# GpSimd's work of the later pairs on VectorE, and M1's two halves a step apart in an attention kernel with two feed-forward layers

## The chip, the cores and the metric

The kernel runs on one core of a Trainium2 chip. The metric is device time in microseconds (us), the median of several executions.

## What is computed

An attention over channels feeds two feed-forward layers. `q`, `k` and `v` are 6016 x 256, the hidden width is 2048.

```python
qn = q / (np.linalg.norm(q, axis=1, keepdims=True) + 1e-06)
kn = k / (np.linalg.norm(k, axis=1, keepdims=True) + 1e-06)
a = softmax(kn.transpose(0, 2, 1) @ qn / tau)     # 256 x 256
x = v @ a
h = x @ w_in;  x = (h * np.clip(h + 3.0, 0.0, 6.0) / 6.0) @ w_out
h = x @ w_in2; r = np.maximum(h, 0.0); out = (r * r) @ w_out2
```

## The kernel before

**Products.** Every product of float32 data is made of three passes (`passes`, lines 308 to 310): an operand is split into a high part (a cast on ScalarE) and a low part (operand minus high part, a subtraction); high times high, low times high and high times low are accumulated in PSUM. The part that is subtracted is called the remainder below.

**Weights.** `v @ a` is never formed: M1 = `a @ w_in` (256 x 2048) is made on the chip and takes the place of the first weights. M1 is made in four parts of 512 hidden columns (`c4` = 0 to 3), each of two halves (`m1_part(c4, i)`, one half of the 256 channels each: six matmuls into a PSUM bank `mp`, then ScalarE's high and VectorE's low parts by `m1_out`, lines 474 and 475). `m1_keep` (line 483) copies both banks out for sums that are formed later.

**Pairs.** The 6016 tokens go in pairs of token groups of 512 (the last pair: 448): pair (j, p), layer j = 0 or 1, p = 0 to 5. The first pair, (0, 0), runs in 32 plain steps of 12 matmuls, in which the parts of M1 and the weights of layer 0 are made ready as well. Step `a` uses part `a // 8` of M1. A part was made at step `x = a + M1_LEAD`, `x` a multiple of 8, both halves one behind the other, that is at steps 6, 14 and 22, and the products that need it are issued at steps 7, 15 and 23.

**Strassen.** The other eleven pairs form the first product of the layer by Winograd's seven products (`strassen`), in eight units (u) of 256 hidden columns. A unit has 45 matmuls: 7 products and 8 groups of the second product, each of three passes. The products need sums and differences of the input blocks (`T1` to `T4`, line 708), split in high and low parts (`hi`, line 711, and `lo`, line 715): eleven GpSimd instructions for each pair, made by `prepare` during the pair before. The weights need such sums too (`m1_sum`, `combine`, line 214; `m1_sums_split`).

**Second weights.** While layer 0 runs, the weights of layer 1 come as 64-bit floats, are converted (`from_float64`, five stages on ScalarE and VectorE, lines 152 to 165), summed (line 214), split (lines 239 to 244 and line 123) and written to DRAM, one `prepare_in` and one `prepare_out` for each u. The sums and remainders were GpSimd's.

**Order.** The program order on each engine is written by hand. `at(place, go)` puts a step at a place; 15 places (`SLOTS`) are one unit of three matmuls a place, place 0 is where the first Strassen pair begins, and `run` issues the steps in order of place. `on_pool` moves a step on until no other GpSimd step lies within 3.2 places:

```python
def on_pool(place, go):
    while any(abs(place - x) < POOL_APART for x in taken):
        place += 0.3
```

In each unit VectorE has eleven instructions of its own: adds of PSUM and a copy (line 761, `h`), the activation (line 775 or 780, `g`) and the remainders (line 123 by way of `split`, `gs`). PE waits for them at fixed places: the first remainder is issued at place 13.8 of a unit and used at 18, the second 17.8 and 21, the third 20 and 24, the fourth 23.4 and 27; the add at 12.6 must have read bank `q` before the product at place 16 adds to it. All engines work through their lists in order. SP issues every transfer.

Of the kernel before, what the change touches and what calls it, by code (L numbers as in the profile page):

```python
# [32 lines left out]
BUSY = (6, 2, 2, 3)  # L33
M1_LEAD = 2
EARLY = 12
# [5 lines left out]
SIGN = -(2 ** 31)  # L41
POOL_APART = 3.2
SLOTS = 15
# [10 lines left out]
def attention_then_two_ffns(  # L54
# [62 lines left out]

    def split(hi, lo, x, part=2, rest=None):

        if part != 1:  # L120
            nc.scalar.copy(hi, x)  # L121
        if part != 0:
            (rest or nc.vector).tensor_tensor(out=lo, in0=x, in1=f32(hi), op=ALU.subtract)  # L123

# [81 lines left out]

    def combine(i, st, a, b):
# [104 lines left out]
    with tc.manual_schedule():  # L312
# [166 lines left out]
        def m1_keep(c4):  # L479
            for k in range(KC):  # L480
                if k == 0:
                    m32[c4] = spare(2 * c4 + 1, f"m32_{c4}").rearrange("p (k f) -> p k f", k=KC)
                nc.scalar.activation(m32[c4][:, k, :], mps.pop((c4, k)), AF.Copy, scale=rsum[k])

        m1_st = {}

        def m1_sum(c4, i):

            if i == 0:
                m1_st[c4] = spare(2 * c4, f"st{c4}").rearrange("p (u a c) -> p u a c", u=2, a=4)  # L490
            m = [m32[c4][:, k, :].rearrange("p (u f c) -> p u f c", u=2, f=2) for k in range(KC)]
            combine(i, m1_st[c4], [[t[:, :, f, :] for f in range(2)] for t in m], lambda t, i: t[:, :, i, :])
# [171 lines left out]

        def on_pool(place, go):
# [12 lines left out]
        def prepare(j, p, start, end):  # L678
# [15 lines left out]
            def combination(r):  # L694
# [18 lines left out]
            def lo(r):  # L713
                h, l = operands[j, p, r]
                nc.gpsimd.tensor_tensor(out=l, in0=ts[r], in1=f32(h), op=ALU.subtract)  # L715

            at(start, load)
            when = {B11: 18.3, B21: 22.3, T2: 26.3}
            for i, r in enumerate((T1, T2)):
                on_pool(start + 12 + 4 * i, lambda r=r: combination(r))  # L720
            for r, x in when.items():
                at(start + x, lambda r=r: hi(r))
                on_pool(start + x + 1.7, lambda r=r: lo(r))
            for i, r in enumerate((T3, T4)):
# [121 lines left out]
        def load_wo2(u):  # L846
            wo_of[u] = wo_tile(u, "wo2_")
            nc.sync.dma_start(out=f32(wo_of[u]), in_=wo2_d[u])

        def prepare_in(u, begin):  # L850
            made = []
            at(begin, lambda: made.extend(second_in(u)))
            for i, x in enumerate((8.7, 9.5, 17.3, 19.4, 22.4)):
                at(begin + x, lambda i=i: made[0][i]())
            x = begin + 22.4
            for i in range(4):
                x = on_pool(x + 3, lambda i=i: made[1](i))
            at(x + 4, lambda: made[2]())
            for i in range(2):
                x = on_pool(x + 6 - 2 * i, lambda i=i: made[3](i))  # L860
            at(x + 6, lambda: made[4]())

        def prepare_out(u, begin):
            made = []
            at(begin, lambda: made.extend(second_out(u)))
            for i, x in enumerate((8.7, 9.5, 17.3, 19.4)):
                at(begin + x, lambda i=i: made[0][i]())
            at(begin + 22.4, lambda: made[0][4](0))
            x = on_pool(begin + 24.5, lambda: made[0][4](1))
            at(x + 6, lambda: made[1]())  # L870
# [83 lines left out]
```

## Time and profile before

| | us |
|---|---|
| median of 3 runs (1062.21 to 1064.5) | 1064.21 |
| the profiled execution | 1063.71 |
| its span, first to last instruction | 1061.9 |
| PE busy | 1042.6 |
| VectorE (DVE) busy | 864.2 |
| ScalarE (ACT) busy | 664.6 |
| GpSimd (POOL) busy | 251.4 |

The span runs from the first to the last instruction of the profiled execution; 1.8 us of its time lie outside. Busy times of matmuls are modelled and overlap; the start of a matmul minus the start of the one before it tells more. Names: acc, y, x, q, h, mp are PSUM banks, gs the split activation, L123 a line of the kernel.

### The profile page before, as it was taken

Reading aid. Unit: us, or ns where it says so; the run is one execution under the profiler, and the core shown is the slowest. Engines: PE = TensorE matmul, PEld = TensorE weight load, DVE = VectorE, ACT = ScalarE, POOL = GpSimd, SP = SyncE. Lnnn points to the kernel's source line nnn. Section 1 sums busy time; section 2 is a strip of 40 time slices with the busy share of each in tenths; the row PEclk is TensorE's granted clock in tenths of the full one; section 3 lists DMA queues with packets and bytes.
Section 4 is the critical chain, followed back from the end, with each engine's and each line's share of the span. In section 5 each row is a group of like instructions: output and inputs, shape, how many; then the busy total and the mean of one; then the engine's idle time right before and its main releaser. Section 6 shows DMA issues by size and latency. Waiting matters only on the chain.

```text
span 1061.9 us, 13045 instructions
## 1 busy us (share of the span) xinstructions
PE 1042.6 (98%) x4630; PEld 865.0 (81%) x4630; DVE 864.2 (81%) x1283; ACT 664.6 (63%) x1200; POOL 251.4 (24%) x211
## 2 busy tenths in 40 slices
PE   9999999999999999999999999999999999999998
PEld 8867777887877888787998888888888888888997
DVE  7898867898898889888889678678778878778766
ACT  6777767777777778776777445455445445545443
POOL 0012244343134133324233022113103104103000
PEclk9999999999999999999999999999999999999999
DMA  9911203102302301320765100100200200200100
GB/s 352 349 42 40 80 1 120 55 20 95 119 0 102 137 31 40 115 90 0 243 236 211 49 1 36 44 1 6 74 1 1 80 1 0 75 1 1 40 1 35
DMA packets 25938, 77.65 MB, mean 73 GB/s; under 512 B 2833, under 2 KB 4881, under 8 KB 25873
## 3 DMA queue, kind: packets, MB, share of 16 engines
q1 hardware_dynamic: 25872, 76.82, 20.4%
q8 instruction: 36, 0.59, 0.2%
q14 instruction: 30, 0.24, 0.1%
HBM read 52.95 MB, written 23.86 MB: 72 GB/s over the span
## 4 chain that ended last, share of the span: by engine, by line
PE 78%; DVE 14%; ACT 6%; issue 2%; POOL 0%; ACTq 0%; POOLq 0%
PE acc L310 13%; PE acc L308 13%; PE acc L309 13%; PE y L308 6%; PE y L309 6%; PE y L310 6%; DVE gs L123 4%; PE s L298 4%; PE q L308 3%; PE q L309 3%; PE q L310 3%; DVE g L775 3%; PE x L308 2%; PE x L310 2%; PE x L309 2%
## 5 line engine op out<-in xcount | busy, mean ns | idle before, releaser
L123 DVE TENSOR_TENSOR gs<-g,gs 128x512 fp32r<-128x512 f32 (+1 forms) x384 | 293.2, 764 | 71.3 <-ACT gs L784 61.7
L310 PE MATMUL acc<-gs,wo 128*128 128x512 f32 (+1 forms) x768 | 298.2, 388 | 5.1 <-DVE gs L123 5.0
L308 PE MATMUL acc<-gs,wo 128*128 128x512 f32 (+1 forms) x768 | 296.6, 386 | 1.6 <-ACT gs L121 1.0
L309 PE MATMUL acc<-gs,wo 128*128 128x512 f32 (+1 forms) x768 | 296.0, 385 | 0.0
L784 ACT CAST gs<-g 128x512 fp32r<-128x512 f32 (+1 forms) x352 | 208.5, 614 | 79.5 <-DVE g L775 55.9
L310 PEld LDWEIGHTS acc<-gs,wo 128*128 128x128 f32 x768 | 144.1, 188 | 39.9 <-DVE gs L123 12.9
L308 PEld LDWEIGHTS acc<-gs,wo 128*128 128x128 f32 x768 | 144.3, 188 | 29.9 <-ACT gs L121 2.2
L309 PEld LDWEIGHTS acc<-gs,wo 128*128 128x128 f32 x768 | 144.3, 188 | 26.7
L715 POOL TENSOR_TENSOR x<-raw,x 128x512 fp32r<-128x512 f32 (+1 forms) x55 | 73.1, 1330 | 368.6 <-ACT x L711 367.1
L780 DVE SCALAR_TENSOR_TENSOR g<-h 128x512 f32<-128x512 f32 (+1 forms) x144 | 120.5, 837 | 0.0
L761 DVE TENSOR_TENSOR h<-q,se 128x512 f32<-128x512 f32 (+1 forms) x88 | 59.5, 676 | 64.3 <-ACT se L757 64.3
L757 ACT COPY se<-y 128x512 f32<-128x512 f32 (+1 forms) x88 | 50.6, 575 | 92.5 <-PE y L310 92.2
L775 DVE SCALAR_TENSOR_TENSOR g<-r,h 128x512 f32<-128x512 f32 (+1 forms) x120 | 104.5, 871 | 3.5 <-ACT r L767 2.9
L757 ACT COPY su<-y 128x512 f32<-128x512 f32 (+1 forms) x88 | 50.8, 577 | 87.4 <-PE y L310 77.1
L767 ACT ACTIVATE r<-h,three 128x512 f32<-128x512 f32 (+1 forms) x120 | 85.6, 714 | 12.5 <-DVE h L761 12.2
L769 ACT ACTIVATE r<-y 128x512 f32<-128x512 f32 (+1 forms) x48 | 28.3, 590 | 56.7 <-PE y L310 56.6
L761 DVE TENSOR_TENSOR h<-q,su 128x512 f32<-128x512 f32 (+1 forms) x88 | 59.2, 673 | 1.0
L761 DVE TENSOR_TENSOR h<-x,sa 128x512 f32<-128x512 f32 (+1 forms) x88 | 59.1, 672 | 0.0
L757 ACT COPY sa<-y 128x512 f32<-128x512 f32 (+1 forms) x88 | 50.7, 576 | 7.0 <-PE y L310 0.9
L780 DVE SCALAR_TENSOR_TENSOR g<-y,r 128x512 f32<-128x512 f32 (+1 forms) x48 | 32.5, 677 | 19.9 <-ACT r L769 19.6
L298 PE MATMUL s<-qk 128*128 128x256 f32 x188 | 42.8, 389 | 0.0
L298 PEld LDWEIGHTS s<-qk 128*128 128x128 f32 x188 | 36.4, 196 | 5.5 <-DMA qk<-in_qk 0.6
(234 smaller groups left out, 1856.8 us busy)
## 6 DMA issues: line engine op xcount, KB each, us to landing
qk<-in_qk SPq DMA_DIRECT2D x23, 512.0 KB, 7.4
wo<-in_w_out SPq DMA_DIRECT2D x16, 512.0 KB, 5.8
wi<-in_w_in SPq DMA_DIRECT2D x10, 512.0 KB, 4.9
x2d<-o SPq DMA_DIRECT2D x20, 256.0 KB, 2.6
raw<-x2d SPq DMA_DIRECT2D x10, 512.0 KB, 5.8
out<-o SPq DMA_DIRECT2D x20, 256.0 KB, 2.3
raw<-in_vt SPq DMA_DIRECT2D x8, 512.0 KB, 6.4
wo2d<-wo2s SPq DMA_DIRECT2D x8, 512.0 KB, 3.0
```

The costliest lines, as they stand in the source:

```text
L123: (rest or nc.vector).tensor_tensor(out=lo, in0=x, in1=f32(hi), op=ALU.subtract)
L298: nc.tensor.matmul(s_ps[i], lhsT=x[:, C + i * P:C + (i + 1) * P], rhs=x[:, :C], start=(t == 0), stop=(t == NT - 1))
L308: nc.tensor.matmul(ps, lhsT=ah, rhs=bh, start=first, stop=False, skip_group_check=more)
L309: nc.tensor.matmul(ps, lhsT=al, rhs=bh, start=False, stop=False, skip_group_check=more)
L310: nc.tensor.matmul(ps, lhsT=ah, rhs=bl, start=False, stop=last, skip_group_check=more)
L715: nc.gpsimd.tensor_tensor(out=l, in0=ts[r], in1=f32(h), op=ALU.subtract)
L757: nc.scalar.copy(s[tag], s["y"])
L761: nc.vector.tensor_tensor(out=s[which], in0=s[ps], in1=s[tag], op=ALU.add)
L767: nc.scalar.activation(s["r" + which], h, AF.Relu, bias=three)
L775: nc.vector.scalar_tensor_tensor(out=g, in0=s["r" + which], scalar=6.0, in1=h, op0=ALU.min, op1=ALU.mult)
L780: nc.vector.scalar_tensor_tensor(out=g, in0=h, scalar=0.0, in1=r, op0=ALU.max, op1=ALU.mult)
L784: nc.scalar.copy(gs[which][0], s["g" + which])
```

## The change

The steps that were GpSimd's go to VectorE, except the sums of parts 0 and 1 of M1 and the operands of pair (0, 1). Of GpSimd's 201 two-input instructions 178 move, 23 stay. They are kept 2.6 places apart in place of 3.2 (3.2 up to place 0). The sums of parts 2 and 3 of M1 begin at places 10 and 34, no longer at -9 and 17. The second weights of u begin at (3.5 + 4.05 u) units in place of (2 + 4.5 u), those of the output at (5.5 + 4.05 u) in place of (4.25 + 4.5 u), and their stages stand closer. With `M1_LEAD` 3 and `x = a + M1_LEAD - i` the first half of a part is made at steps 5, 13 and 21, the second at 6, 14 and 22 as before. No instruction is added or left out on any engine beside the move.

```diff
-M1_LEAD = 2
+M1_LEAD = 3
-POOL_APART = 3.2
+APART = 2.6
+APART_FIRST = 3.2
...
-        nc.gpsimd.tensor_tensor(out=b(st, to), in0=x, in1=y, op=op)
+        eng.tensor_tensor(out=b(st, to), in0=x, in1=y, op=op)
...
-            nc.gpsimd.tensor_tensor(out=lo[:, a, :], in0=w, in1=f32(hi[:, a, :]), op=ALU.subtract)
+            nc.vector.tensor_tensor(out=lo[:, a, :], in0=w, in1=f32(hi[:, a, :]), op=ALU.subtract)
...
-            split(t[:, 0, :], t[:, 1, :], x, part, rest=nc.gpsimd)
+            split(t[:, 0, :], t[:, 1, :], x, part)
...
+        def idle_first(first):
+            return nc.gpsimd if first else nc.vector
...
-            split(hi, lo, m1_st[c4][:, u, :, :], part, rest=nc.gpsimd)
+            split(hi, lo, m1_st[c4][:, u, :, :], part, idle_first(c4 < 2))
...
-            while any(abs(place - x) < POOL_APART for x in taken):
+            while any(abs(place - x) < (APART if place > 0 else APART_FIRST) for x in taken):
...
-                nc.gpsimd.tensor_tensor(out=to, in0=x, in1=y, op=ALU.subtract)
+                idle_first((j, p) == (0, 1)).tensor_tensor(out=to, in0=x, in1=y, op=ALU.subtract)
...
-                nc.gpsimd.tensor_tensor(out=l, in0=ts[r], in1=f32(h), op=ALU.subtract)
+                idle_first((j, p) == (0, 1)).tensor_tensor(out=l, in0=ts[r], in1=f32(h), op=ALU.subtract)
...
-        for c4, x in enumerate((-100, -72, -9, 17)):
+        for c4, x in ((0, -100), (1, -72), (2, 10), (3, 34)):
...
+        def converted(begin, make):
+            made = []
+            at(begin, lambda: made.extend(make()))
+            at(begin + 8.7, lambda: made[0][0]())
+            x = begin + 8.7
+            for i in range(1, 4):
+                x = extra(x + (1.6, 1.6, 1.3)[i - 1], lambda i=i: made[0][i]())
+            return made, x
...
-            prepare_in(u, (2 + 4.5 * u) * SLOTS)
-            prepare_out(u, (4.25 + 4.5 * u) * SLOTS)
+            prepare_in(u, (3.5 + 4.05 * u) * SLOTS)
+            prepare_out(u, (5.5 + 4.05 * u) * SLOTS)
...
-            x = a + M1_LEAD
-            if x % 8 == 0 and 0 < x < 32:
-                for i in range(KC):
+            for i in range(KC):
+                x = a + M1_LEAD - i
+                if x % 8 == 0 and 0 < x < 32:
                     m1_part(x // 8, i)
-                m1_keep(x // 8)
+                    if i == KC - 1:
+                        m1_keep(x // 8)
```

The first place is VectorE's list in the first unit of pair (0, 3), from its first add `h11` to the remainder `gs11`. Names: `gs`, `g`, `h` and their blocks (11, 22, 12, 21), layer, pair and unit; `o` is an eviction of the pair before, `ta`/`tb` the conversion of second weights, `x0_3_6` the low part of operand T4 of pair (0, 3), `wa2s` the low parts of second weights. Before:

```order
L761 TENSOR_TENSOR h110_3_0_3137<-x0_3_0_3121,sa0_3_0_3113 128x512
L123 TENSOR_TENSOR gs120_2_7_3135<-g120_2_7_3119,gs120_2_7_3135 128x512
L775 SCALAR_TENSOR_TENSOR g210_2_7_3150<-r210_2_7_3139,h210_2_7_3128 128x512
L123 TENSOR_TENSOR gs210_2_7_3157<-g210_2_7_3150,gs210_2_7_3157 128x512
L775 SCALAR_TENSOR_TENSOR g110_3_0_3173<-r110_3_0_3164,h110_3_0_3137 128x512
L160 SCALAR_TENSOR_TENSOR tawi2_3_3109<-tbwi2_3_3110,tawi2_3_3109 128x512
L581 TENSOR_SCALAR o0_2_1_0_3179<-acc0_2_1_0_2446 128x512
L165 ISA tawi2_3_3109<-tawi2_3_3109,tywi2_3_3111 128x1024
L761 TENSOR_TENSOR h220_3_0_3197<-q0_3_0_3159,se0_3_0_3186 128x512
L123 TENSOR_TENSOR gs110_3_0_3192<-g110_3_0_3173,gs110_3_0_3192 128x512
```

Now:

```order
L771 TENSOR_TENSOR h110_3_0_3130<-x0_3_0_3113,sa0_3_0_3105 128x512
L124 TENSOR_TENSOR gs120_2_7_3128<-g120_2_7_3111,gs120_2_7_3128 128x512
L785 SCALAR_TENSOR_TENSOR g210_2_7_3143<-r210_2_7_3132,h210_2_7_3117 128x512
L725 TENSOR_TENSOR x0_3_6_3141<-raw0_3_1_2750,x0_3_6_3141 128x512
L124 TENSOR_TENSOR gs210_2_7_3150<-g210_2_7_3143,gs210_2_7_3150 128x512
L785 SCALAR_TENSOR_TENSOR g110_3_0_3166<-r110_3_0_3157,h110_3_0_3130 128x512
L245 TENSOR_TENSOR wa2s21_3034<-w32_2_2771,wa2s20_3033 128x384
L590 TENSOR_SCALAR o0_2_1_0_3172<-acc0_2_1_0_2423 128x512
L245 TENSOR_TENSOR wa2s21_3034<-w32_2_2771,wa2s20_3033 128x512
L771 TENSOR_TENSOR h220_3_0_3189<-q0_3_0_3152,se0_3_0_3178 128x512
L124 TENSOR_TENSOR gs110_3_0_3183<-g110_3_0_3166,gs110_3_0_3183 128x512
```

Between the two ends stood eight instructions and now stand nine: a remainder of operand T4 and two of the second weights came in, two stages of a conversion went to other places. The whole unit, up to the next `h11`, had 15 instructions and now has 18. In the 40 units of pairs (0, 1) to (0, 5) the list had 511 and now has 633.

The second place is VectorE's list in the first pair around part 2 of M1: `wa1_2l` and `a21_2` are its low parts, read from bank `mp2_0` (first half) and `mp2_1` (second half), `g0_0_7` and `gs0_0_7` the activation of step 14, `wo1_4` and `ta`/`tb` conversions. Before:

```order
L123 TENSOR_TENSOR gs0_1_6_977<-g0_1_6_974,gs0_1_6_977 128x512
L123 TENSOR_TENSOR wo1_4_993<-tawo1_4_912,wo1_4_993 128x512
L622 SCALAR_TENSOR_TENSOR g0_0_7_1001<-r0_0_7_999,h0_0_7_980 128x512
L156 TENSOR_SCALAR tawi1_6_966<-wi1_6_883 128x512
L157 TENSOR_SCALAR tbwi1_6_967<-tbwi1_6_967 128x512
L123 TENSOR_TENSOR gs0_0_7_1006<-g0_0_7_1001,gs0_0_7_1006 128x512
L475 SCALAR_TENSOR_TENSOR wa1_2l_1024<-mp2_0_1016,rs0_507,wa1_2h_1023 128x2x128
L475 SCALAR_TENSOR_TENSOR a21_2_1025<-mp2_0_1016,rs0_507,a21_2_1025 128x256
L475 SCALAR_TENSOR_TENSOR wa1_2l_1024<-mp2_1_1030,rs1_521,wa1_2h_1023 128x2x256
```

Now:

```order
L124 TENSOR_TENSOR gs0_1_6_977<-g0_1_6_974,gs0_1_6_977 128x512
L476 SCALAR_TENSOR_TENSOR wa1_2l_995<-mp2_0_987,rs0_507,wa1_2h_994 128x2x128
L476 SCALAR_TENSOR_TENSOR a21_2_996<-mp2_0_987,rs0_507,a21_2_996 128x256
L124 TENSOR_TENSOR wo1_4_1007<-tawo1_4_912,wo1_4_1007 128x512
L631 SCALAR_TENSOR_TENSOR g0_0_7_1015<-r0_0_7_1013,h0_0_7_980 128x512
L157 TENSOR_SCALAR tawi1_6_966<-wi1_6_884 128x512
L158 TENSOR_SCALAR tbwi1_6_967<-tbwi1_6_967 128x512
L124 TENSOR_TENSOR gs0_0_7_1020<-g0_0_7_1015,gs0_0_7_1020 128x512
L476 SCALAR_TENSOR_TENSOR wa1_2l_995<-mp2_1_1030,rs1_521,wa1_2h_994 128x2x256
```

The two low parts of the first half have moved ahead by five instructions; only the low part of the second half is left where all three stood.

## Rows read from the trace of the kernel before

**Rows 1.** The page, part 1: busy time, share of the span and instructions of each engine.
```profile
PE 1042.6 (98%) x4630; PEld 865.0 (81%) x4630; DVE 864.2 (81%) x1283; ACT 664.6 (63%) x1200; POOL 251.4 (24%) x211
```

**Rows 2.** Windows by stage: length, then busy us (instructions) of PE, PEld, DVE, ACT, POOL, PEclk, DMA.
```profile
55.30:158.40 103.10, 98.83 (x409) 75.03 (x410) 86.51 (x141) 75.79 (x130) 27.45 (x23) 1.00 0.13 41
158.40:241.90 83.50, 81.87 (x359) 66.63 (x358) 70.67 (x99) 62.25 (x112) 33.60 (x29) 1.00 0.17 62
241.90:326.00 84.10, 81.65 (x358) 66.41 (x357) 72.76 (x104) 63.55 (x113) 25.03 (x22) 1.00 0.20 68
326.00:411.70 85.70, 83.07 (x359) 67.96 (x358) 74.25 (x105) 63.17 (x113) 28.60 (x23) 0.98 0.23 83
411.70:496.50 84.80, 83.67 (x363) 67.26 (x362) 72.76 (x105) 63.24 (x115) 27.66 (x25) 1.00 0.22 77
496.50:571.90 75.40, 74.64 (x361) 66.91 (x360) 67.55 (x102) 57.12 (x110) 27.69 (x23) 1.00 0.58 198
...
653.00:734.70 81.70, 81.70 (x362) 67.64 (x361) 63.37 (x91) 40.72 (x75) 15.60 (x11) 1.00 0.09 26
```

**Rows 3.** Waits of PE, 158.4 to 571.9: us in total, times, longest.
```profile
PE acc L310 <- DVE gs L123: 3.7, 5, 1.8
PE q L308 <- DVE h L761: 3.6, 2, 2.6
```

**Rows 4.** Timelines around 335 us: POOL, then DVE, then PE (start, us, engine, line).
```profile
332.30 1.73 POOL L244 TENSOR_TENSOR wa2s<-w,wa2s 128x512 fp32r<-128x512 f32 x1
334.00 1.73 POOL L123 TENSOR_TENSOR wo2s<-tawo,wo2s 128x512 fp32r<-128x512 f32 x1
...
332.81 1.77 DVE L775 SCALAR_TENSOR_TENSOR g<-r,h 128x512 f32<-128x512 f32 x1
334.51 1.77 DVE L160 SCALAR_TENSOR_TENSOR tawi<-tbwi,tawi 128x512 int32<-128x512 int32 x1
...
336.80 0.67 DVE L165 CUSTOM_DVE_ANT_0 tawi<-tawi,tywi 128x1024 uint16<-128x1024 uint16 x1
337.40 0.68 DVE L761 TENSOR_TENSOR h<-q,se 128x512 f32<-128x512 f32 x1
...
335.12 0.39 PE L310 MATMUL y<-x,wa_0h 128*128 128x512 f32 x1
338.13 0.79 PE L308 MATMUL q<-x,wa_0h 128*128 128x512 f32 x1 [2.63 <-DVE h L761]
338.72 0.63 PE L309 MATMUL q<-x,wa_0l 128*128 128x512 f32 x1
```

**Rows 5.** Groups of DVE by line and shape: count, busy us, mean ns, idle before.
```profile
L780 DVE SCALAR_TENSOR_TENSOR g<-h 128x512 f32<-128x512 f32 x120 | 105.6, 880 | 0.0
```

**Rows 6.** The page, part 5: GpSimd's remainders of the operands.
```profile
L715 POOL TENSOR_TENSOR x<-raw,x 128x512 fp32r<-128x512 f32 (+1 forms) x55 | 73.1, 1330 | 368.6 <-ACT x L711 367.1
```

**Rows 7.** Waits of DVE, 158.4 to 571.9: us in total, times, longest.
```profile
DVE gs L123 <- ACT gs L784: 22.3, 34, 0.8
```

**Rows 8.** Waits of PE, 55.3 to 158.4: us in total, times, longest.
```profile
PE h L308 <- ACT wa_3h L474: 0.4, 1, 0.4
PE h L308 <- ACT wa_2h L474: 0.3, 1, 0.3
PE h L309 <- DVE wa_2l L475: 0.3, 1, 0.3
PE h L309 <- DVE wa_1l L475: 0.3, 1, 0.3
PE h L309 <- DVE wa_3l L475: 0.3, 1, 0.3
```

**Rows 9.** Timeline of PE where part 2 of M1 is first used.
```profile
108.01 0.40 PE L310 MATMUL h<-x,wa_2h 128*128 128x512 f32 x1
108.74 0.49 PE L308 MATMUL h<-x,wa_2h 128*128 128x512 f32 x1 [0.33 <-ACT wa_2h L474]
109.52 0.50 PE L309 MATMUL h<-x,wa_2l 128*128 128x512 f32 x1 [0.29 <-DVE wa_2l L475]
```

More of the change, by code (lines that the diff above doesn't have):

```diff
@@ L116, in f32, with split @@
         return x.bitcast(F32)
-    def split(hi, lo, x, part=2, rest=None):
+    def split(hi, lo, x, part=2, eng=nc.vector):
         if part != 1:
@@ L122, in split @@
         if part != 0:
-            (rest or nc.vector).tensor_tensor(out=lo, in0=x, in1=f32(hi), op=ALU.subtract)
+            eng.tensor_tensor(out=lo, in0=x, in1=f32(hi), op=ALU.subtract)
     def wa_tiles(c4, name):
@@ L205, in attention_then_two_ffns, with combine @@
     wo2_d = [dram.tile([P, 2, 512], F32, name=f"wo2d{u}") for u in range(NU)]
-    def combine(i, st, a, b):
+    def combine(i, st, a, b, eng=nc.vector):
         (a11, a21_), (a12, a22) = a
@@ L481, in m1_keep, with beside @@
                 if k == 0:
-                    m32[c4] = spare(2 * c4 + 1, f"m32_{c4}").rearrange("p (k f) -> p k f", k=KC)
+                    m32[c4] = beside(c4, 1).rearrange("p (k f) -> p k f", k=KC)
                 nc.scalar.activation(m32[c4][:, k, :], mps.pop((c4, k)), AF.Copy, scale=rsum[k])
         m1_st = {}
+        def idle_first(first):
+            return nc.gpsimd if first else nc.vector
+        def beside(c4, i):
+            return spare(2 * c4 + i, f"m32_{c4}{i}")
         def m1_sum(c4, i):
             if i == 0:
-                m1_st[c4] = spare(2 * c4, f"st{c4}").rearrange("p (u a c) -> p u a c", u=2, a=4)
+                m1_st[c4] = beside(c4, 0).rearrange("p (u a c) -> p u a c", u=2, a=4)
             m = [m32[c4][:, k, :].rearrange("p (u f c) -> p u f c", u=2, f=2) for k in range(KC)]
-            combine(i, m1_st[c4], [[t[:, :, f, :] for f in range(2)] for t in m], lambda t, i: t[:, :, i, :])
+            combine(i, m1_st[c4], [[t[:, :, f, :] for f in range(2)] for t in m], lambda t, i: t[:, :, i, :], idle_first(c4 < 2))
         def m1_sums_split(c4, u, part):
             hi, lo = (t[:, u, S1:, :] for t in wa1[c4])
-            split(hi, lo, m1_st[c4][:, u, :, :], part, rest=nc.gpsimd)
+            split(hi, lo, m1_st[c4][:, u, :, :], part, idle_first(c4 < 2))
         def m1_part(c4, i):
@@ L663, in attention_then_two_ffns, with extra @@
         taken = []
-        def on_pool(place, go):
-            while any(abs(place - x) < POOL_APART for x in taken):
+        def extra(place, go):
+            while any(abs(place - x) < (APART if place > 0 else APART_FIRST) for x in taken):
                 place += 0.3
@@ L719, in prepare @@
             for i, r in enumerate((T1, T2)):
-                on_pool(start + 12 + 4 * i, lambda r=r: combination(r))
+                extra(start + 12 + 4 * i, lambda r=r: combination(r))
             for r, x in when.items():
                 at(start + x, lambda r=r: hi(r))
-                on_pool(start + x + 1.7, lambda r=r: lo(r))
+                extra(start + x + 1.7, lambda r=r: lo(r))
             for i, r in enumerate((T3, T4)):
-                on_pool(start + 32 + 4 * i, lambda r=r: combination(r))
+                extra(start + 32 + 4 * i, lambda r=r: combination(r))
             first_pair = {T3: 0.3, T1: -14.5, B22: 4.3, T4: -10.5}
@@ L730, in prepare @@
                 at(after, lambda r=r: hi(r))
-                on_pool(after + 1.7, lambda r=r: lo(r))
+                extra(after + 1.7, lambda r=r: lo(r))
         def strassen(j, p, u, at0):
@@ L848, in load_wo2 @@
             nc.sync.dma_start(out=f32(wo_of[u]), in_=wo2_d[u])
-        def prepare_in(u, begin):
[L851 to L855, printed above, removed]
+        def converted(begin, make):
[6 more added lines that the diff above has]
+            return made, x
+        def prepare_in(u, begin):
+            made, x = converted(begin, lambda: second_in(u))
+            at(x + 1.6, lambda: made[0][4]())
+            x += 4
             for i in range(4):
-                x = on_pool(x + 3, lambda i=i: made[1](i))
-            at(x + 4, lambda: made[2]())
+                x = extra(x, lambda i=i: made[1](i)) + 0.7
+            at(x + 1, lambda: made[2]())
+            x += 3.5
             for i in range(2):
-                x = on_pool(x + 6 - 2 * i, lambda i=i: made[3](i))
-            at(x + 6, lambda: made[4]())
+                x = extra(x, lambda i=i: made[3](i))
+            at(x + 4, lambda: made[4]())
         def prepare_out(u, begin):
[L864 to L870, printed above, removed]
+            made, x = converted(begin, lambda: second_out(u))
+            at(x + 1.6, lambda: made[0][4](0))
+            x = extra(x + 3, lambda: made[0][4](1))
+            at(x + 4, lambda: made[1]())
         for u in range(NU):
-            prepare_in(u, (2 + 4.5 * u) * SLOTS)
-            prepare_out(u, (4.25 + 4.5 * u) * SLOTS)
+            prepare_in(u, (3.5 + 4.05 * u) * SLOTS)
+            prepare_out(u, (5.5 + 4.05 * u) * SLOTS)
         last = unit_at[1, 0]
```

6 lines of the change are left out of this document (3 added, 3 removed).

## The prediction

> **What bounds the kernel now.** The first view is the page's busy times [rows 1]: PE is busy for 98% of the span, so the time is PE's issue rate plus whatever PE waits. The second view, the windows by stage [rows 2], says where it waits. Pair (1, 1), a pair of 512 columns in layer 1, takes 81.7 us and PE is busy in all of them; that is the floor of such a pair. The same work in layer 0 takes 83.5, 84.1, 85.7 and 84.8 us: 1.8, 2.4, 4.0 and 3.1 us over the floor. Pair (0, 5) has narrower columns and no twin among the rows; PE is idle for at least 75.4 - 74.64 = 0.8 us of it. Layer 0 behind the first pair therefore loses 12.1 us. The first stretch, 55.3 to 158.4, has 103.10 - 98.83 = 4.3 us of plain idle time. Layer 1 has nothing to give.
>
> The third view, the waits of PE in layer 0 [rows 3], says for whom: the remainder `gs` (3.7 us) and the add that frees bank `q` (3.6 us), both on VectorE. The fourth, the timelines around 335 us [rows 4], says why VectorE was late. GpSimd ran two remainders of second weights back to back, 1.73 us each. VectorE's two instructions beside them took 1.77 us each; the same kind takes 0.68 us alone. PE issued at 335.12 and then not until 338.13. The next matmul came 0.59 us later, where 0.23 is usual (81.7 us over 360 matmuls): the mean granted clock of that pair is 0.98, in the others 1.00 [rows 2], so after this stop the lower of the two levels was granted for a while. The groups of VectorE by shape [rows 5] show the same as a mean: `g<-h`, with both inputs in SBUF, takes 880 ns.
>
> So a GpSimd instruction holds up a VectorE instruction by about 1.77 - 0.68 = 1.1 us. Done by VectorE itself, it occupies VectorE from one start to the next: 336.80 to 337.40, 0.60 us [rows 4]. That trade is the case for the change.
>
> **The change, part by part.**
>
> *What VectorE gets in layer 0.* The five stages from 158.4 to 571.9 hold 122 GpSimd instructions (29 + 22 + 23 + 25 + 23) and 515 of VectorE with 358 us busy [rows 2]. At 0.60 us each the 515 would take 309 us, so some 49 us are hold-up. Of the 122, about 75 are full width: 75 x 0.60 = 45 us. Eight of 384 columns cost 3.6 us by their share, eight of 256 between 2.4 and 4.8 us. The 32 sums of 128 columns have no row on VectorE: at least a quarter of 0.60, at most all of it, 4.8 to 19.2 us. The whole is 56 to 73 us; I take 60, near the lower end, because a narrow instruction is nearer to its share of columns plus a small start cost. So 358 us become 309 + 60 = 369, while PE's floor for the stage is 413.5 - 12.1 = 401 us. VectorE stays under PE, at 92% (95% at the upper end), and what can hold up one instruction shrinks from 1.1 us at a moment that nobody planned to 0.60 us at a place in the list.
>
> *What stays of the loss.* An average of 92% hides uneven units. The first unit of pair (0, 3) has 18 instructions in the new list: 17 x 0.60 + 0.45 = 10.7 us against 81.7 / 8 = 10.2 us of PE. Four pairs begin so, because evictions, operands and conversions meet there, and each puts VectorE 0.5 us behind. The slack between a remainder and its use is 3.2 to 4.2 places, 2.2 to 2.9 us at 0.68 us a place, which should take this; I still charge the four 0.5 us, 2.0 us, for what queues up behind. Layer 0 then gains 12.1 - 2.0 = **10.1 us**. Its bounds: 14 us, if nothing is left and (0, 5) loses as much as the 512 pairs, and 5 us, if half stays and the four units cost 1 us more than I charge.
>
> *Layer 1.* 11 moved instructions a pair cost 11 x 0.60 = 6.6 us of VectorE, beside 63.37 us of 81.7 [rows 2]. PE did not wait there even with the hold-up. Cost: 0, hidden by some 18 us of VectorE's idle time; without that cover 6.6 us a pair.
>
> *M1's halves.* In the first pair the second low part of M1 is late for the product that needs it. The rows name 1.6 us in five waits [rows 8]. From start to start it is more: around part 2 the matmuls stand 0.73 and 0.78 us apart where 0.23 is usual [rows 9], 1.05 us where the waits name 0.6. Scaled alike, 1.6 becomes 2.8 us. In the new list the two low parts of the first half stand five instructions earlier, so only one is left between the second half and the product. I take **2.5 us**, bounds 1.0 (the stall just moves to step 5) and 2.8. What the step is moved past: six matmuls and two casts come one step earlier, the mp bank is held a step longer, and the next user of that bank is three steps on. SP's order of loads around it is the same.
>
> *The rest of the first pair.* 23 GpSimd instructions stay, nearly all of the 23 in 55.3 to 158.4 [rows 2], so its other idle time stays: 0. SP's queue: the same transfers, those of the second weights in another rhythm, writes now behind VectorE's remainders in place of GpSimd's. The last ends well before layer 1 loads it: 0.
>
> *Sum.* The profiled execution took 1063.7 us with a span of 1061.9. 1063.7 - 10.1 - 2.5 = 1051.1. The median of the runs is 0.5 us above this execution, so I predict **1051.5 us**.
>
> **The rivals.**
>
> *Half the loss stays.* The same list on one engine puts the delay elsewhere: moved work is as long as the hold-up it replaces (60 against 49 us), so VectorE is as full as before. For: the busy sum even rises a little. Against: the losses came from single delays of over 1 us in a row, and none of that size is left. Layer 0 gains 6 us: 1063.7 - 6 - 2.5 + 0.5 = 1055.7.
>
> *VectorE becomes the bound.* If each moved or old instruction kept VectorE for its whole 0.68 us, the 633 instructions of the new list would take about 309 x 0.68/0.60 + 60 x 0.68/0.60 = 418 us where PE needs 401 and the stage took 413.5. Then layer 0 loses 4.5 us and M1 gives 2.5: about 1066. The rows speak against it, as starts lie 0.60 us apart. The Trainium skill, VectorE: DVE Perf Modes, section The DRAIN you can't avoid, says that the next operation does not start until the pipe is empty, which would be this case; the same section adds that one which is not held starts earlier, and the trace agrees with the addition (0.60 against 0.68).
>
> *A wait takes the place of the lock.* GpSimd's remainders waited 367.1 us for ScalarE's cast [rows 6], which cost nothing as GpSimd had nothing else. In VectorE's list everything behind such a wait stands still, the next activation and the add for bank `q` first. VectorE's own remainders waited 22.3 us in 34 cases for that cast [rows 7], 0.66 us each. 63 of the moved instructions of layer 0 are remainders with a cast ahead. If all were late by that much, VectorE would need 369 + 41 = 410 us against 401, and PE would stand in every full unit. It decides from the point where 13 us, twenty of these waits, reach PE; with thirty, 20 us, the time is 1064.2 + 7 = **1071**. Against: the casts are listed 1.7 places (1.2 us) ahead and take 0.6. The Trainium skill, Perfetto Trace Analysis, section Optimizing Scalar/DVE Operations, says that work of a saturated VectorE may go to ScalarE or even GpSimd, the reverse of this change, and that between VectorE and GpSimd it might not help; by the first half of that one would expect this rival, and the hold-up of 1.1 us speaks for the second.
>
> *The halves do nothing.* M1's stall moves to where the first half is made: 1054.
>
> **How the numbers follow.** Forecast 0.55 (1047 to 1054, from gains of 14 + 2.8 and of 8 + 2 off the median), half stays 0.22 (1054 to 1059), the halves do nothing 0.06 (in between), VectorE the bound 0.09 (1058 to 1067), the wait 0.08 (1062 to 1075). Range 1046 to 1060, the lower end 1 us under the best case for scatter of the runs. About 0.2%, 2.1 us, is what a measurement of this kernel can tell from no change. Faster: 0.55 + 0.22 + 0.06 + 0.04 = 0.87; same 0.05; slower 0.08.
>
> **What would show it.** Right: the pairs of layer 0 take about 82 to 82.5 us, `g<-h` falls from 880 ns to about 0.68 us, the clock reads 1.00 in each, and no product of M1 waits for `wa_`. VectorE's busy time stays within 20 us of 864. Wrong: PE's waits for `gs` or `h` in the first units of pairs (0, 2) to (0, 5) of a microsecond or more, VectorE idle before remainders with ScalarE named, or pairs of layer 1 over 82 us.

## The result and the profile after

The changed kernel takes **1050.24 us** (median of 4 runs, 1049.97 to 1050.44); the kernel before, on the same chip, 1064.36 (4 runs). The ratio is 0.9861, 95% interval 0.9848 to 0.9875: faster by 14.1 us. The forecast was 1051.5. The profiled execution took 1050.34 with a span of 1048.6.

The page of the changed kernel, part 1, against [rows 1]:

```profile
PE 1036.5 (99%) x4630; PEld 865.8 (83%) x4630; DVE 863.9 (82%) x1461; ACT 665.5 (63%) x1200; POOL 29.4 (3%) x33
```

178 instructions have gone from GpSimd to VectorE, and VectorE's busy time is 863.9 us where it was 864.2. The moved work took up just the time that the hold-ups had taken: GpSimd's instructions had made VectorE's own ones longer.

The windows by stage of the changed kernel, columns as in [rows 2]: the first pair, pairs (0, 1) to (0, 5), and (1, 1).

```profile
56.10:158.10 102.00, 98.36 (x409) 75.44 (x410) 85.79 (x141) 75.33 (x130) 25.58 (x21) 1.00 0.13 42
158.10:238.30 80.20, 79.52 (x351) 65.57 (x350) 67.78 (x118) 60.90 (x106) 2.59 (x2) 1.00 0.14 47
238.30:319.90 81.60, 81.60 (x362) 67.61 (x361) 75.18 (x132) 65.03 (x116) 0.00 (x0) 1.00 0.25 88
319.90:401.50 81.60, 81.60 (x362) 67.61 (x361) 74.49 (x130) 64.43 (x115) 0.00 (x0) 1.00 0.24 87
401.50:483.40 81.90, 81.86 (x362) 67.36 (x361) 74.24 (x131) 63.93 (x114) 0.00 (x0) 1.00 0.24 86
483.40:558.50 75.10, 75.10 (x362) 67.51 (x361) 67.52 (x125) 58.03 (x111) 0.00 (x0) 1.00 0.55 192
...
639.70:721.30 81.60, 81.60 (x361) 67.61 (x360) 63.77 (x102) 40.49 (x74) 0.00 (x0) 1.00 0.08 27
```

Pairs (0, 2) and (0, 3) take 81.60 us, as long as pair (1, 1) of layer 1, and PE is busy in all of it. The five pairs of layer 0 took 413.5 us and take 400.4: 13.1 gained. Layer 1 to the end took 490.0 and takes 490.1 (1048.6 - 558.5). The first pair is 1.1 us shorter and begins 0.8 us later. 13.1 + 1.1 - 0.8 - 0.1 = 13.3, the difference of the spans. Behind the long stop of [rows 4] the granted clock of the kernel before was 0.50 from 337.7 to 341.1 us, the lower of the two levels; in the changed kernel it is 1.00 in every stage shown.

Waits of PE in layer 0 of the changed kernel, 158.1 to 558.5, against [rows 3]: all that is left.

```profile
PE y L309 <- ACT se L767: 0.7, 1, 0.7
```

VectorE's groups by shape (columns as in [rows 5]): first two of the kernel before, then the changed kernel (L725 and L215 are moved work). Its longest waits in layer 0 follow.

```profile
L775 DVE SCALAR_TENSOR_TENSOR g<-r,h 128x512 f32<-128x512 f32 x96 | 83.3, 868 | 2.9 <-ACT r L767 2.3
L761 DVE TENSOR_TENSOR h<-q,se 128x512 f32<-128x512 f32 x72 | 49.5, 688 | 53.1 <-ACT se L757 53.1
...
L790 DVE SCALAR_TENSOR_TENSOR g<-h 128x512 f32<-128x512 f32 x120 | 82.1, 684 | 0.0
L785 DVE SCALAR_TENSOR_TENSOR g<-r,h 128x512 f32<-128x512 f32 x96 | 65.9, 687 | 3.4 <-ACT r L777 3.4
L725 DVE TENSOR_TENSOR x<-raw,x 128x512 fp32r<-128x512 f32 x40 | 27.4, 685 | 0.0
L215 DVE TENSOR_TENSOR w<-w 128x128 f32<-128x128 f32 x32 | 9.1, 285 | 0.0
```

```profile
DVE gs L124 <- ACT gs L794: 12.7, 26, 0.7
DVE h L771 <- ACT se L767: 11.1, 19, 1.1
```

`g<-h` fell from 880 to 684 ns [rows 5]. That group is line 780 of the kernel before, the activation of layer 1, where PE did not wait; its counterpart in layer 0 is `g<-r,h`, which fell from 868 to 687 ns. Both have all operands in SBUF. The add `h<-q,se` reads a PSUM bank and took 688 ns before as well, though 14 of its 32 in layer 0 ran beside a GpSimd instruction: GpSimd lengthened only instructions whose operands were all in SBUF. The moved remainders of operands never wait (last column 0.0), and the wait of `gs` for its cast shrank from 22.3 to 12.7 us [rows 7].

VectorE's timeline of the changed kernel in the first unit of pair (0, 3), where [rows 4] showed 1.77 us instructions:

```profile
326.67 0.69 DVE L590 TENSOR_SCALAR o<-acc 128x512 f32<-128x512 f32 x1
327.27 0.69 DVE L245 TENSOR_TENSOR wa2s<-w,wa2s 128x512 fp32r<-128x512 f32 x1
327.87 0.69 DVE L771 TENSOR_TENSOR h<-q,se 128x512 f32<-128x512 f32 x1
328.48 0.69 DVE L124 TENSOR_TENSOR gs<-g,gs 128x512 fp32r<-128x512 f32 x1
```

Starts lie 0.60 us apart, the moved L245 among them.

M1 is another matter. Timelines of the changed kernel around part 2: ScalarE, VectorE, then PE where the part is first used [rows 9].

```profile
103.84 0.46 ACT L475 ACTIVATE wa_2h<-mp,rs 128x256 fp32r<-128x256 f32 x1
105.08 0.47 ACT L475 ACTIVATE a<-mp,rs 128x256 fp32r<-128x256 f32 x1 [0.78 <-DVE wa_2l L476]
...
107.95 0.68 ACT L475 ACTIVATE wa_2h<-mp,rs 128x512 fp32r<-128x512 f32 x1
...
104.57 0.48 DVE L476 SCALAR_TENSOR_TENSOR wa_2l<-mp,rs,wa_2h 128x256 fp32r<-128x256 f32 x1
105.59 0.48 DVE L476 SCALAR_TENSOR_TENSOR a<-mp,rs,a 128x256 fp32r<-128x256 f32 x1 [0.54 <-ACT a L475]
...
108.69 0.74 DVE L476 SCALAR_TENSOR_TENSOR wa_2l<-mp,rs,wa_2h 128x512 fp32r<-128x512 f32 x1
...
108.01 0.40 PE L311 MATMUL h<-x,wa_2h 128*128 128x512 f32 x1
108.68 0.50 PE L309 MATMUL h<-x,wa_2h 128*128 128x512 f32 x1 [0.28 <-ACT wa_2h L475]
109.49 0.50 PE L310 MATMUL h<-x,wa_2l 128*128 128x512 f32 x1 [0.30 <-DVE wa_2l L476]
```

PE still stands 0.67 and 0.81 us where 0.23 is usual. Over parts 1 to 3 the excess between starts was 0.51 + 1.06 + 1.08 = 2.65 us and is 0.51 + 1.03 + 0.96 = 2.50. The first half's parts are made 2.5 us earlier (103.84 where they began at 106.38), and the second half's come when they always came: 107.95 and 108.69, before 108.00 and 108.72. What the step between needs has moved behind the first half; the sum of work ahead of the second half is the same. The rows also show something that the prediction did not look at. ScalarE's second cast waits 0.78 us for VectorE's first low part, of which it needs no value: both only read bank `mp`, and the program's semaphore lets one read after the other. VectorE's second low part does need that cast, and waits 0.54 us for it. The engines take turns.

### The profile page after: what moved, and what is told of

Read it like the earlier page. It is cut to its first block, busy times and chain, and to the rows that moved or that the text cites. A ratio compares the mean times of both kernels' runs of the same rounds, so it can differ in the third digit from the quotient of the medians.

```text
span 1048.6 us, 12978 instructions
## 1 busy us (share of the span) xinstructions
PE 1036.5 (99%) x4630; PEld 865.8 (83%) x4630; DVE 863.9 (82%) x1461; ACT 665.5 (63%) x1200; POOL 29.4 (3%) x33
## 4 chain that ended last, share of the span: by engine, by line
PE 90%; DVE 6%; ACT 3%; DMA 1%; issue 1%; SPq 0%
PE acc L311 15%; PE acc L310 15%; PE acc L309 15%; PE y L309 7%; PE y L310 7%; PE y L311 7%; PE q L309 4%; PE q L311 4%; PE q L310 4%; PE s L299 3%; PE x L311 2%; PE x L309 2%; PE x L310 2%; DVE gs L124 1%; DVE g L631 1%; DMA qk<-in_qk 1%
## 5 line engine op out<-in xcount | busy, mean ns | idle before, releaser
L124 DVE TENSOR_TENSOR gs<-g,gs 128x512 fp32r<-128x512 f32 (+1 forms) x384 | 260.6, 679 | 55.7 <-ACT gs L794 45.9
L790 DVE SCALAR_TENSOR_TENSOR g<-h 128x512 f32<-128x512 f32 (+1 forms) x144 | 97.0, 673 | 0.0
L785 DVE SCALAR_TENSOR_TENSOR g<-r,h 128x512 f32<-128x512 f32 (+1 forms) x120 | 80.8, 674 | 3.8 <-ACT r L777 3.8
L296 DVE TENSOR_TENSOR scratch<-sq,scratch 128x512 f32<-128x512 f32 x47 | 29.3, 684 | 7.7 <-ACT sq L295 7.6
```

Of the source, the lines that this page charges most:

```text
L124: eng.tensor_tensor(out=lo, in0=x, in1=f32(hi), op=ALU.subtract)
L296: nc.vector.tensor_tensor(out=sums[t % 2], in0=sq, in1=sums[t % 2], op=ALU.add)
L785: nc.vector.scalar_tensor_tensor(out=g, in0=s["r" + which], scalar=6.0, in1=h, op0=ALU.min, op1=ALU.mult)
L790: nc.vector.scalar_tensor_tensor(out=g, in0=h, scalar=0.0, in1=r, op0=ALU.max, op1=ALU.mult)
```

## The experiments

The theory from the prediction is that GpSimd's hold-ups are what makes VectorE late, so that moving the work is what helps. The first rival is that the new places are what helps: the same change spreads the conversions and the second weights. A second question is what M1's halves do.

For one measure across all kernels the window below runs from PE's first product of pair (0, 1) to that of pair (1, 0), the same 1800 matmuls in each; its ends are rounded to 0.1 us. Each ratio is against the kernel before on the same chip (medians 1064.36 to 1065.54 us).

| kernel | us, ratio to before (95%) | window | VectorE busy in it |
|---|---|---|---|
| before | 1 | 415.60 | 360.01 |
| changed | 1050.24, 0.9861 (0.9848 to 0.9875) | 402.60 | 361.03 |
| `engine_alone` | 1052.80, 0.9877 (0.9863 to 0.9891) | 403.40 | 361.21 |
| `places_alone` | 1054.05, 0.9889 (0.9875 to 0.9903) | 406.00 | 348.97 |
| `spread_alone` | 1055.10, 0.9908 (0.9892 to 0.9923) | 407.30 | 353.70 |
| `pool_reads` | 1062.97, 0.9981 (0.9971 to 0.9991) | 414.17 | 393.83 |
| `vector_plus1` | 1054.85, 0.9905 (0.9890 to 0.9921) | 405.60 | 383.11 |

### M1's halves, alone and undone

`m1_alone` is the kernel before with the halves a step apart, `m1_undone` the changed kernel with both halves at steps 6, 14 and 22 again.

```diff
-M1_LEAD = 2
+M1_LEAD = 3
...
-            x = a + M1_LEAD
+            for i in range(KC):
+                x = a + M1_LEAD - i
...
```

> The kernel before with M1's halves a step apart and nothing else. The step of the prediction (the second low part is late because the first half's work stands right ahead of it) expects 2.5 us less, 1061.9. The rival, that VectorE and ScalarE are behind PE by the work in their lists and that the same work still stands ahead of the second half, expects no change, within 0.5 us of 1064.4, and the matmuls at the first use of parts 1 to 3 as far apart as before (0.73 and 0.78 us at part 2).

> The changed kernel with both halves of M1 in one step again. The step of the prediction expects 2.5 us more, 1052.7; the rival (work in the lists) no change, within 0.5 us of 1050.2.

`m1_alone` took 1065.10 us, ratio 0.9992 (0.9983 to 1.0001); `m1_undone` 1050.55, ratio 0.9861 (0.9844 to 0.9877). The halves are worth nothing that these medians can tell, with GpSimd's hold-ups or without. In the traces PE's first pair is 0.5 us shorter with the halves apart, both times (102.9 to 102.4 and 102.3 to 101.8 us), a fifth of the 2.5 us expected.

### The engine alone, the places alone

`engine_alone` has the places of before and the work on VectorE; `places_alone` the places of after and the work on GpSimd.

```diff
 engine_alone, from the kernel before:
-        nc.gpsimd.tensor_tensor(out=b(st, to), in0=x, in1=y, op=op)
+        eng.tensor_tensor(out=b(st, to), in0=x, in1=y, op=op)
...
 places_alone, from the changed kernel:
-            nc.vector.tensor_tensor(out=lo[:, a, :], in0=w, in1=f32(hi[:, a, :]), op=ALU.subtract)
+            nc.gpsimd.tensor_tensor(out=lo[:, a, :], in0=w, in1=f32(hi[:, a, :]), op=ALU.subtract)
...
-            split(t[:, 0, :], t[:, 1, :], x, part)
+            split(t[:, 0, :], t[:, 1, :], x, part, nc.gpsimd)
...
-            return nc.gpsimd if first else nc.vector
+            return nc.gpsimd
```

> The places and M1 of the kernel before, with the same 178 instructions on VectorE. If the hold-up is the cause, most of the gain is here: 1050 to 1054, more than the changed kernel only by what uneven places cost. If the places make the gain, 1059 or more, with PE waiting for VectorE in layer 0.

> The changed kernel's places (2.6 apart, second weights at the new starts, M1's sums and halves) with all the moved work on GpSimd again. If the hold-up of VectorE by GpSimd makes the loss of layer 0, it comes back: 12 us more than the changed kernel, 1060 to 1065, and VectorE's instructions of 1.7 us are there again. If the new places make the gain, it stays at 1050 to 1053.

The engine alone gives 12.2 us of the window, the places alone 9.6, both together 13.0. `engine_alone` lies in the range on record for the hold-up; `places_alone`, 1054.05, between the two ranges on record. Two groups of VectorE (the first is of layer 1, the second of layer 0) and PE's waits in the window, `places_alone`:

```profile
L790 DVE SCALAR_TENSOR_TENSOR g<-h 128x512 f32<-128x512 f32 x120 | 105.5, 879 | 0.0
L785 DVE SCALAR_TENSOR_TENSOR g<-r,h 128x512 f32<-128x512 f32 x96 | 88.6, 923 | 5.6 <-ACT r L777 5.5
```

```profile
PE y L309 <- ACT se L767: 0.7, 1, 0.7
PE acc L311 <- DVE gs L124: 0.4, 1, 0.4
```

PE's waits in `engine_alone`:

```profile
PE y L308 <- ACT se L760: 0.7, 1, 0.7
PE acc L310 <- DVE gs L123: 0.6, 1, 0.6
PE y L308 <- ACT sa L760: 0.6, 1, 0.6
```

In `places_alone` most of the hold-up is still there: `g<-r,h` takes 923 ns where it took 868 before. How much, the busy times tell. The instructions that VectorE had before the change take 302 us from start to start in the window of the changed kernel; what the table has above that is hold-up, 58 us before and 47 in `places_alone`. A fifth of the hold-up went, and three quarters of the loss (13.0 us over the changed kernel to 3.4); the waits of [rows 3] are all but gone. So the loss does not follow the amount of hold-up: it was large where conversions, evictions and second weights lay close together. The crowd alone did not make it either. `engine_alone` keeps it, and pair (0, 3), where its two stops of 0.6 us lie, is 2.2 us longer (83.8 for 81.6). Its window is only 0.8 us longer because pair (0, 5) is 1.3 us shorter (73.7 for 74.9), without a stop in either kernel: most matmuls stand 0.203 us apart there in place of 0.207, and why stays open. Most of the rest of the 2.6 us lies in the first pair, 103.0 us for 101.8. In the kernel before it took both to lose 13 us, and either part of the change removes most.

### Which of the places

`spread_alone` is the kernel before, GpSimd and all, with the extra steps 2.6 apart as in the change: the conversion's stages take part in the search for a free place, and the steps of the second weights follow them and stand as close as in the change. The starts of second weights and sums and M1 stay.

```diff
-POOL_APART = 3.2
+APART = 2.6
+APART_FIRST = 3.2
...
-            for i, x in enumerate((8.7, 9.5, 17.3, 19.4, 22.4)):
-                at(begin + x, lambda i=i: made[0][i]())
...
+            for i in range(1, 4):
+                x = extra(x + (1.6, 1.6, 1.3)[i - 1], lambda i=i: made[0][i]())
...
```

> The kernel before, all its GpSimd work on GpSimd and its old starts; only the stages of the second weights' conversion are kept 2.6 places away from GpSimd's steps and stand as close as in the changed kernel. Theory 1 (crowding: a hold-up costs PE time only where a conversion meets GpSimd's steps, so that several delays add up): most of the 11 us that the new places gave without the move come from here, 1053 to 1057. Theory 2 (the later and denser starts even out the units): 1061 to 1065.

It gives 8.3 of the 9.6 us of window, in the range on record for crowding. One conversion stage of VectorE over the whole run, before and in `spread_alone`:

```profile
L160 DVE SCALAR_TENSOR_TENSOR tawo<-tbwo,tawo 128x512 int32<-128x512 int32 x16 | 13.0, 810 | 0.0
...
L161 DVE SCALAR_TENSOR_TENSOR tawo<-tbwo,tawo 128x512 int32<-128x512 int32 x16 | 10.9, 683 | 0.0
```

VectorE's conversion stages hardly meet GpSimd's remainders any more (14 of the 64 in the window were lengthened before, 2 here), while 52 of the 58 us of hold-up remain. The run does not separate that from the closer steps of the second weights. The later starts and the remaining places are worth 1.3 us, of which 0.8 lie in pair (0, 5).

### Hold-ups put back, work added

`pool_reads` is the changed kernel with a GpSimd read of 128x352 beside 120 of VectorE's remainders in layer 0; its result is used nowhere. `vector_plus1` repeats one full add on VectorE in each unit of layer 0.

```diff
 pool_reads:
+    idle = const.tile([P, 352], mybir.dt.bfloat16, name="idle")
...
+                if j == 0 and which != "21":
+                    x = f32(gs[which][0])[:, :352]
+                    nc.gpsimd.tensor_tensor(out=idle, in0=x, in1=x, op=ALU.subtract)
                 split(*gs[which], s["g" + which], 1)
...
 vector_plus1:
+            if j == 0:
+                for place_ in (8.4,):
+                    at(at0 + place_, lambda: nc.vector.tensor_tensor(out=s["11"], in0=s["x"], in1=s["sa"], op=ALU.add))
```

> The changed kernel with 120 more GpSimd instructions in layer 0, three in each unit, which read 352 columns of SBUF beside VectorE's remainders and write a buffer that nobody reads; VectorE's list is the same. If each hold-up costs PE by itself, they bring back some 10 us (1058 to 1062). If only crowded ones do, evenly placed ones cost 1 to 4 us (1051 to 1054), though g<-r,h or gs show more than 0.69 us in the mean.

> The changed kernel with one more full-width addition on VectorE in each of the 40 units of layer 0 (the add h11 a second time, at place 8.4). 40 x 0.60 = 24 us more: 383 of 400 us. If VectorE is free until it is full, less than 2 us more (1050 to 1052). If VectorE is near its bound already, most of the 24 us show, 1060 to 1074.

PE's waits in the window and a piece of the timelines (POOL, then DVE) of `pool_reads`:

```profile
PE acc L312 <- DVE gs L125: 3.6, 10, 0.7
PE q L310 <- DVE h L772: 1.0, 2, 0.7
...
```

```profile
252.97 1.95 POOL L800 TENSOR_TENSOR idle<-gs 128x352 bf16<-128x352 f32 x2 [4.40 <-ACT gs L795]
...
253.25 1.04 DVE L125 TENSOR_TENSOR gs<-g,gs 128x512 fp32r<-128x512 f32 x1
254.22 1.25 DVE L167 CUSTOM_DVE_ANT_0 tawo<-tawo,tywo 128x1024 uint16<-128x1024 uint16 x1
255.40 0.68 DVE L772 TENSOR_TENSOR h<-x,sa 128x512 f32<-128x512 f32 x1
```

PE's waits of `vector_plus1` in its window:

```profile
PE q L309 <- DVE h L771: 0.9, 4, 0.2
...
PE acc L311 <- DVE gs L124: 0.2, 1, 0.2
```

GpSimd's two reads lengthen the VectorE instructions beside them (1.04 and 1.25 us), and the 120 reads bring back 11.6 of the 13.0 us; ten of PE's stops name `gs`. No wait of ScalarE or VectorE in the window names GpSimd, so it is not that the reads keep the `gs` buffers. Hold-ups do it without the crowd, then, where they are laid on the remainders that PE waits for and VectorE's list is as full as in the changed kernel. Both runs miss their ranges on record: 1062.97 lies just above the first one, 1054.85 between the two. The listed add brings 22.1 us more busy time and costs 3.0 us of window (1.7 us more lie ahead of the first pair, which begins later in that run), the reads 32.8 us and 11.6. Whether a hold-up costs more per microsecond than listed work stays open: the amounts differ, and VectorE is at 94% (add) and 95% (reads) of the window, so the last 10 us may weigh more than the first.

### The rest of GpSimd's work

`all_vector` moves the 23 instructions of the first pair as well.

```diff
-            return nc.gpsimd if first else nc.vector
+            return nc.vector
```

> The changed kernel with the last 23 instructions of GpSimd (sums of parts 0 and 1 of M1, operands of pair (0, 1)) on VectorE as well. If the first pair loses by the hold-up, its stalls at 95.8 and 122 to 124 us go: 1 to 2 us less, 1048.5 to 1049.5. If VectorE's list is what PE waits for there, 23 more instructions of 0.3 to 0.6 us add 5 to 12 us: 1055 to 1062.

1049.56 us (1048.75 to 1050.72), ratio 0.9858 (0.9840 to 0.9875): not told apart from the changed kernel. It lies 0.06 us above the range on record for stalls that go. The window is 401.70, 0.9 us less, but all of that is in pair (0, 5), whose matmuls stand 0.203 us apart here too (73.9 us for 74.9); in the first pair some stops of PE go (at 65, 96 and 122 to 124 us) and others come (at 92, 103 and 134).

### Why M1's second half is late

`m1_earlier` puts both halves one more step ahead. `casts_first` lists both casts of a half ahead of VectorE's low parts, so that the engines change over once in place of three times. `casts_first_earlier` has both edits, and `best` both and `all_vector`'s.

```diff
-M1_LEAD = 3
+M1_LEAD = 4
```

```diff
             for x, (hi, lo) in to:
                 nc.scalar.activation(hi, x, AF.Copy, scale=rsum[k])
+            for x, (hi, lo) in to:
                 nc.vector.scalar_tensor_tensor(
```

> The changed kernel with both halves of each part of M1 one more step earlier (the second half at steps 5, 13 and 21, where 6, 14 and 22 was). Theory 'a step's work stands ahead': the second half's parts are late because ScalarE and VectorE must first finish the parts of the first half and the activation of the step between, so one step (12 matmuls, 2.7 us) more takes the stalls where the parts are first used (0.51 + 1.03 + 0.96 = 2.5 us of gaps between starts in the profile of the changed kernel) away: 1047.7 to 1049, ratio to the changed kernel 0.998 to 0.9985. Rival 'the lateness moves along with the halves' (something else fills the lists there): 1050.2, no change, the gaps stay at about 2.5 us. Rival 'bank mp is held too long': stalls of PE at the halves' own matmuls in place of the old ones, 1050 to 1053.

> The changed kernel with ScalarE's casts of a half listed as a pair ahead of VectorE's two low parts, where cast, low part, cast, low part alternate now. Theory 'a step's work stands ahead': in the profile of the changed kernel the second cast of a half stands 0.78 us behind VectorE's first low part, and VectorE's second low part 0.54 us behind that cast; without the alternation 0.8 us of ScalarE's and 0.5 of VectorE's come free ahead of the activation of the step, so the gaps at the parts' first use fall from 2.5 to between 0.5 and 1.7 us: 1048.2 to 1049.5. Rival 'the engines are not what is late': 1050.2 and gaps of 2.5 us. Rival 'the alternation is not the order of the list but of the bank's readers': the 0.78 us wait stays in the profile though the list no longer asks for it, 1050.2.

> The two edits before together. If both take the same lateness away, this is as fast as the better of the two, 1047.7 to 1049; if each takes only a part, it is below both; if neither does anything, 1050.2.

> The two edits together, and GpSimd's last 23 instructions (sums of parts 0 and 1 of M1, operands of the second pair) on VectorE as well. These 23 alone gave 1049.6 in an earlier run (0.7 us under the changed kernel). If the gains add: 1047 to 1048.5. If VectorE, now also with GpSimd's part of the first pair in its list, is late for the parts again: 1049 to 1051.

| kernel | us | ratio to before (95%) |
|---|---|---|
| `m1_earlier` | 1051.89 | 0.9873 (0.9860 to 0.9887) |
| `casts_first` | 1047.13 | 0.9828 (0.9814 to 0.9841) |
| `casts_first_earlier` | 1051.41 | 0.9865 (0.9851 to 0.9880) |
| `best` | 1049.78 | 0.9855 (0.9839 to 0.9870) |

`m1_earlier`, the longest of PE's waits in the first pair (56 to 158.5 us; the other two are 0.5 and 0.4 us), and the timelines around its third stop, ACT, DVE, then PE:

```profile
PE mp L309 <- ACT wi1h L122: 6.7, 3, 2.5
...
```

```profile
125.30 0.62 ACT L122 CAST gs<-g 128x512 fp32r<-128x512 f32 x1 [2.31 <-DVE g L631]
125.90 0.62 ACT L122 CAST wi1h<-tawi 128x512 fp32r<-128x512 f32 x1
...
125.19 0.68 DVE L166 CUSTOM_DVE_ANT_0 tawi<-tawi,tywi 128x1024 uint16<-128x1024 uint16 x1
...
123.76 0.39 PE L311 MATMUL mp<-wi1l,eth 128*128 128x512 f32 x1
126.57 0.50 PE L309 MATMUL mp<-wi1h,eth 128*128 128x512 f32 x1 [2.42 <-ACT wi1h L122]
```

No product waits for parts 1 to 3 of M1 any more, as the theory had it. But the halves' own matmuls now wait for the weights `wi1h`, whose conversion ends at 125.9 us (125.19 + 0.68) and is cast behind it. 6.7 us of new waits stand against the 2.5 us of gaps and some other stops that went: PE's first pair, from its first product to that of pair (0, 1), takes 103.1 us in place of 101.8. The last of the cases on record had the place and the time (1050 to 1053) and not the cause: it is not the bank that is late but the weights. GpSimd, which still works in the first pair, lengthened two stages of that conversion (0.93 and 1.51 us, 0.42 when undisturbed); it is not the main cause, since `best`, below, has nothing on GpSimd there and still waits 5.4 us.

`casts_first`, the same place as in the changed kernel above:

```profile
102.82 0.47 ACT L475 ACTIVATE wa_2h<-mp,rs 128x256 fp32r<-128x256 f32 x1
103.19 0.47 ACT L475 ACTIVATE a<-mp,rs 128x256 fp32r<-128x256 f32 x1
...
103.69 0.48 DVE L477 SCALAR_TENSOR_TENSOR wa_2l<-mp,rs,wa_2h 128x256 fp32r<-128x256 f32 x1
104.09 0.47 DVE L477 SCALAR_TENSOR_TENSOR a<-mp,rs,a 128x256 fp32r<-128x256 f32 x1
...
107.21 0.39 PE L309 MATMUL h<-x,wa_2h 128*128 128x512 f32 x1
107.86 0.50 PE L310 MATMUL h<-x,wa_2l 128*128 128x512 f32 x1 [0.26 <-DVE wa_2l L477]
```

The wait of 0.78 us is gone, and with it PE's stop for the second half's cast; one of 0.65 - 0.23 = 0.42 us is left. Over parts 1 to 3 the excess is 0 + 0.42 + 0.40 = 0.82 us, 1.7 less. PE's first pair takes 99.3 us where it took 101.8, and the window of layer 0 is 402.70 as before this edit (402.60). The 1047.13 us are below the range on record (1048.2 to 1049.5): the first pair gained 2.5 us, and the parts account for 1.7 of them; some stops elsewhere in the pair are shorter too. This is the fastest kernel of the study. `casts_first_earlier` and `best` have the waits for `wi1h` again (4.9 and 5.4 us) and lose what they gain: the first pair takes 104.1 and 101.7 us. Behind two of these waits in `casts_first_earlier`, and one in `best`, the granted clock was 0.50 for some 3.3 us. With 1051.41 us `casts_first_earlier` fits none of its cases on record; `best` has the time of its second case, though not the cause, which is `wi1h` here too. `casts_first` with `all_vector` alone, and `casts_first` with the halves together again, were not tried.

## Why the prediction was right

**The pairs of layer 0: right in place and mechanism, 3.0 us too small.** It took 10.1 us of the 12.1 that PE lost; the stage gained 13.1, within the bounds of 5 to 14. Two terms were mis-sized.

The larger one is the loss itself. The stages of [rows 2] are cut by time and do not all hold the same matmuls. From first product to first product, 360 matmuls each, pairs (0, 1) to (0, 4) took 84.3, 85.0, 86.2 and 84.5 us, which is 13.6 over four times 81.6, where the prediction added up 11.3. They now take 82.6, 81.6, 81.6 and 81.9. Of the 1.3 us left, 0.7 is the stop of pair (0, 1) for `se`, which the kernel before has too.

The other is "I still charge the four 0.5 us, 2.0 us, for what queues up behind". The slack took all of it: the full units open pairs (0, 2) to (0, 5), and PE is busy in 81.60 of 81.60 us of the first two.

The price of the moved work was right: 60 us were taken, and from start to start the moved instructions occupy VectorE for 60 us in the changed window. The 309 us for the rest were 302, and so the hold-up was 58 us and not 49.

**"That trade is the case for the change": half of it.** The engine alone gives 12.2 of 13.0 us, so the move suffices. But it is no saving of VectorE's time, 60 us of work for 58 of hold-up. The 1.1 us that it took for a hold-up is a long one, read around 335 us; the mean over 122 GpSimd instructions is 58 / 122 = 0.5 us, about what the work costs VectorE itself. What changed is that 57 instructions of VectorE in the window took over a microsecond before and none does now, as the prediction had it at the end of its paragraph on VectorE's list. The mean that it read for this, `g<-h` [rows 5], is of layer 1. And it costed the new places at nothing of their own, while they alone give 9.6 us with 47 us of hold-up still there.

**M1's halves: wrong, 2.5 us too much.** The failed step: "so only one is left between the second half and the product. I take 2.5 us". It counted what stands between the two halves' parts. What counts is what stands ahead of the second half's parts, and the move leaves that alone. The rival "The halves do nothing", given 0.06, is what happened to this term in number; the stall did not move to where the first half is made, as it had it, but stayed where it was. The layer's surplus of 3.0 us paid for the 2.5. That the sum came out 1.3 us from the measurement is luck: two errors of opposite sign. (The terms of the sum give 1051.6, not 1051.5.)

**Layer 1 and the rest of the first pair: right.** 490.0 and 490.1 us with VectorE at 63.8 of 81.6 us in pair (1, 1). The first pair's longer stops remain but for one at 95.3 us (0.89 to 0.42 us over the usual spacing).

**The rivals.** Half stays: out, next to nothing stays. VectorE the bound: out, starts 0.60 us apart. The Trainium skill, VectorE: DVE Perf Modes, section The DRAIN you can't avoid, has both cases, and the rows above show the one where the next operation is not held. A wait in place of the lock: out, the waits of VectorE for the cast became fewer. The signs named for "right" held (684 ns, clock 1.00, DVE within 1 us of 864), except two: the full pairs take 81.6 to 81.9 us, where 82 to 82.5 was named, and products still wait for `wa_`.

## What to carry to other kernels

A GpSimd instruction with operands in SBUF was paid for here by the VectorE instruction that it met, if that one had all its operands in SBUF too (0.68 became up to 1.8 us). Look at where such pairs lie in VectorE's list: 58 us of hold-up cost 13.0 us in a crowd, 47 us cost 3.4 in loose order, and spacing out the list may be had without moving work at all. When a producer is late, count all that its engine must do ahead of it: putting one of two producers earlier moves the queue, it does not shorten it, and going further early meets the next input that is not there. Where two engines read one PSUM bank, and the program lets them take turns, list each engine's reads together: with the reads alternating, one engine waited for a result that it did not need.

## What was not expected of the hardware

VectorE's busy time did not move by 178 added instructions (863.9 against 864.2 us), because instructions with all operands in SBUF became shorter (`g<-r,h` of 868 ns became 687, `g<-h` of 880 became 684): the page's busy share hid the hold-ups as work. Adds that read a PSUM bank were not lengthened (688 and 690 ns). The 0.78 us that ScalarE waited for VectorE at bank `mp` is a wait for the program's semaphore and shows no limit of the bank; whether the two may read it side by side no run here shows.
